# Attention beside an MLP on one core: w2's parts in fourteen tiles, the output weights split on GpSimd, other orders for attention

## The chip, the core and the metric

The kernel runs on one core of a Trainium2 chip. The core has five engines with a queue each: TensorE (PE; its weight loads are shown apart as PEld), VectorE (DVE), ScalarE (ACT), GpSimd (POOL) and SyncE (SP), which here issues nearly all DMAs. Each engine takes its instructions in order, and an instruction that has to wait holds up all behind it on that engine. Matmuls write to PSUM, which has eight banks of 128 partitions by 512 float32. The metric is the time of the kernel on the device in microseconds, less being better.

## The reference

Attention with 16 query heads that share one head of keys and values, and an MLP, both on the normalized input, are added to it. S = 2048 rows, D = 448, 16 heads of 28, F = 1792, all in float32:

```python
def _A_ref(x, wq, wk, wv, wo):
    q = (x @ wq).reshape(B, S, H, Dh).transpose(0, 2, 1, 3)
    k = x @ wk
    v = x @ wv
    scores = jnp.einsum("bhqd,bkd->bhqk", q, k) * (Dh ** -0.5)
    p = _softmax(scores, axis=-1)
    o = jnp.einsum("bhqk,bkd->bhqd", p, v)
    return o.transpose(0, 2, 1, 3).reshape(B, S, H * Dh) @ wo

def _B_ref(x, w1, b1, w2, b2):
    y = _layernorm(x, axis=-1)
    h = _gelu(jnp.einsum("bsd,df->bsf", y, w1) + b1)
    return jnp.einsum("bsf,fd->bsd", h, w2) + b2

xn = _layernorm(x, axis=-1)
return x + _A_ref(xn, A_wq, ...) + _B_ref(xn, B_w1, ...)
```

## The kernel before

The order of the work on every engine is the order in which the program writes it; nothing reorders it. Most products keep float32 accuracy by splitting both factors into a high part in a shorter format (fp32r) and the low rest: high x high, high x low and low x high are summed.

There are three stages. The first (to about 63 us) loads and normalizes the rows in four chunks of 512, splits the weights, and makes queries, keys and values; queries go to DRAM (`qd`) by DMA from tiles named `qe`.

**The MLP** (63 to 349 us) walks through 56 slots (loop at L635): four chunks of 512 rows by 14 tiles `ft` of the hidden width. In slot n, `mlp1` (L557) makes a hidden tile: eleven matmuls, then ScalarE, VectorE and GpSimd apply GELU and split the result into `hh` and `hl`. `mlp2` (L575) of two slots before multiplies `hh` and `hl` with w2: twelve matmuls. During the first chunk (c = 0), w2 is split too: `w2_split(s)` (L377) takes tiles 2s and 2s+1, 128 x 896 numbers. ScalarE writes the high part into `w2h`, VectorE the low part into `w2l`, and the load of part s+2 is issued (two buffers). It is called behind `mlp1` in slot 0 and in the odd slots 3, 5, ... 13 for s = 0 to 6, so that the parts s are first read by `mlp2` in slot 2s+2. `w2h` and `w2l` are one tile each of 14 x 448 columns; they lie in memory that the first stage's tiles held before.

**Attention** (from 349 us) has 16 units: four chunks of 512 queries by four groups of four heads. A unit walks through 16 key tiles of 128 keys. The steps of a unit are written out in a string of `ORDERS` (L34), where each word is a step:

- `s` with a number is `scores` (L612) of one key tile: three rounds of four matmuls (one for each head, on a quarter of the array's rows each) into four banks, then exponents on ScalarE (L625) into a tile `p`. The bits of the number say which neighbouring heads are joined in one instruction: bit 0 joins heads 0 and 1, bit 1 heads 1 and 2, bit 2 heads 2 and 3. So s6 makes one of 512 and one of 1536 columns, s5 two of 1024, s2 512, 1024, 512, s0 four of 512. Heads whose banks are not neighbours in number (7 and 0) aren't joined.
- `P` with a number is `weighted` (L791): the values are multiplied with the exponents of so many key tiles (`pv`, L735), summed in one bank, and VectorE adds the bank to `oc` (L733) or copies it for a unit's first (L731). A key tile is two rounds of four matmuls, on a quarter of the array's columns each.
- `m` searches the next unit's shift (`find_max`, L540: one matmul, L523, then four instructions on VectorE and a small DMA to the next unit's queries). `Q` is one output tile of the chunk before (`out_tile`, L703: twelve matmuls, L701). `T` and `E` are the same for the last chunk at the end of the kernel.

Banks are handed out in a ring of eight: four for a score step, one for each P, m, Q and T. A step waits for the bank that was handed out eight places before. Order 0 is for units 0 to 3, order 1 for units 4 to 14, order 2 for unit 15. Two score steps are made ahead of unit 0, so a unit's orders begin with the scores of its key tile 2 and end with the next unit's tile 1. A finished unit's normalization (`norm_jobs`, L711) is done by VectorE behind the first and third P of the next one, with one subtraction on GpSimd (`otl`, L723).

The output weights `wo` are loaded by four DMAs on SyncE's queue (L678) between the MLP and attention; the loads of unit 1's queries (`load_unit`, L533) stand behind them. `split_out` (L681) splits them on VectorE with a copy and a subtraction of 128 x 1792 numbers, behind the third step of unit 0. The parts are first read by Q in unit 4.

Of the kernel before, what the change touches and what calls it, by code (L numbers as in the profile page):

```python
# [11 lines left out]
F32R = mybir.dt.float32r  # L12
I32 = mybir.dt.int32
AF = mybir.ActivationFunctionType
ALU = mybir.AluOpType
# [3 lines left out]
P = 128  # L19
S, D, H, DH, F = 2048, 448, 16, 28, 1792  # L20
# [5 lines left out]
NF = F // P  # L26
# [4 lines left out]
MLP_ORDER = 1, 2, 3, 0  # L31
HD = D // 2
WEIGHTS = 7
ORDERS = ("s5 P1 s6 s6 P2 s6 s5 P2 s4 s1 m P2 s6 P1 s6 s5 P2 s6 s6 P2 s6 s5 P2 s6 s4 P2",  # L34
          "s5 P1 s6 s6 P2 s6 s5 P2 s6 s6 P2 s6 s5 P2 s2 s2 P2 s2 m Q s2 s6 P3 s6 s4 P2",
          "s5 P1 s6 s6 P2 s6 s5 P2 s6 s6 P2 s6 s5 P2 s2 s2 P2 s2 m Q s2 s6 P2 T T T E3")
FIRST_BANK = 0
LIMITS = 0.25, 2.0 ** 40

# [2 lines left out]
def block_kernel(ctx, tc, x, wq, wk, wv, wo, w1, b1, w2, b2, out):  # L42
    nc = tc.nc
    pe, act, dve, pool = nc.tensor, nc.scalar, nc.vector, nc.gpsimd
    ctx.enter_context(tc.manual_schedule())

    def f(t):
        return t.bitcast(F32)
# [60 lines left out]
    def bank(n, shape=(P, CW)):  # L109
        t = banks[0:shape[0], n, 0:shape[1] * (shape[2] if len(shape) > 2 else 1)]  # L110
        return t.rearrange("p (a b) -> p a b", b=shape[2]) if len(shape) > 2 else t
# [158 lines left out]
    def line(t):  # L270
        lines[t] = keep.tile([P, D], F32, name="a", bufs=4)
        nc.sync.dma_start(lines[t], xv[:, t, :])
# [99 lines left out]
    def w2_load(s):  # L372
        raw = rawtile([P, 2, D])
        nc.sync.dma_start(raw, w2[2 * s * P:(2 * s + 2) * P, :].rearrange("(b p) n -> p b n", p=P))
        wl_q.append(raw)

    def w2_split(s):  # L377
        raw = wl_q.pop(0)
        ab = slice(2 * s, 2 * s + 2)

        act.activation(w2h[:, ab, :], raw, AF.Copy, scale=0.5)
        dve.scalar_tensor_tensor(w2l[:, ab, :], raw, 0.5, f(w2h[:, ab, :]), op0=ALU.mult, op1=ALU.subtract)  # L382
        if s + 2 < NF // 2:
            w2_load(s + 2)

# [81 lines left out]
    for c in range(NCH):  # L467
        if c + 1 < NCH:
            center, turn = norm_parts(c + 1, False)
        for i in range(4):  # L470
# [4 lines left out]
            low = None  # L475
            if evac is not None:
                vt, low = evac()
# [3 lines left out]
            for part, k in (("", "c0 c1", "t0 c2 t1 c3", "t2 t3") if c == 0 else  # L481
                            ("c0 c1", "t0 c2 t1 c3", "t2 t3", "") if c + 1 < NCH else [""] * 4)[i].split():
                if part == "t" and low is not None:
                    low()
                    low = None
# [9 lines left out]
            if i in ((1, 3), (1, 2), (1, 3), (0, 2))[c]:  # L495
                n = 2 * c + (i - 1 if c == 1 else i // 2 if c == 3 else i // 3)
# [16 lines left out]
    def clear_q():  # L513
        both = xt_p.tile([P, 4, CW], F32R, name="xh")
        pool.memset(f(both), 0.0)
        qst.extend((both[:, 0:2, :], both[:, 2:4, :]))
# [16 lines left out]
    def load_unit(u):  # L533
        c, g = units[u]
        qs = qss[u] = qst[u % 2]
        for j in range(4):
            rs = slice(DH * (4 * g + j), DH * (4 * g + j + 1))
            nc.sync.dma_start(f(qs[32 * j:32 * j + DH, :, :]), qd[rs, :, c * CW:(c + 1) * CW])

    def find_max(u):  # L540
        mr = keep.tile([P, CW // 32], F32, name="mr", bufs=2)
        block_max(u, kd, mr)
        shift_rows(u, mr)
# [5 lines left out]

    ph1b = ExitStack()  # L550
    hp = ph1b.enter_context(tc.tile_pool(name="hp", bufs=3))
    w2h = hp.tile([P, NF, D], F32R, name="w2h", bufs=1)
    w2l = hp.tile([P, NF, D], F32R, name="w2l", bufs=1)

    hs, m2s = {}, {}

    def mlp1(c, ft):  # L557
        yh, yl = xts[MLP_ORDER[c], True]
        ph = spare()
        fs = slice(ft * P, (ft + 1) * P)  # L560
        proj(ph, lambda b: w1h[:, b, fs], lambda b: w1l[:, b, fs], yh, yl)
        hx = hrp.tile([P, CW], F32, name="hx", bufs=2)
        hz = hrp.tile([P, CW], F32, name="hz", bufs=2)
        act.activation(hx, ph, AF.Identity, bias=b1t[:, ft:ft + 1])  # L564
        act.activation(hz, ph, AF.Square, bias=b1s[:, ft:ft + 1], scale=GELU[0] ** 0.5)  # L565
        dve.scalar_tensor_tensor(hz, hz, 1.0, hx, op0=ALU.add, op1=ALU.mult)  # L566
        act.activation(hz, hz, AF.Tanh, scale=GELU[1])  # L567
        dve.scalar_tensor_tensor(hx, hz, 1.0, hx, op0=ALU.add, op1=ALU.mult)  # L568
        hh = hrp.tile([P, CW], F32R, name="hh")
        hl = hrp.tile([P, CW], F32R, name="hl")  # L570
        dve.tensor_copy(hh, hx)  # L571
        pool.tensor_sub(hl, hx, f(hh))  # L572
        hs[c, ft] = (hh, hl)

    def mlp2(c, ft, then=None):  # L575
        if ft == 0:
            m2s[c] = [bank(CT + k, (P, D)) for k in range(CT)]
        m2 = m2s[c]
        hh, hl = hs.pop((c, ft))
        terms = ((hh, w2h), (hh, w2l), (hl, w2h))  # L580
        parted = c == 0 and ft == 0
        if parted:
            for k in range(CT):
                for i, (h, w) in enumerate(terms[:2]):
                    pe.matmul(m2[k], h[:, k * P:(k + 1) * P], w[:, ft, :], start=(i == 0), stop=False)
        for k in range(CT):
            for i, (h, w) in enumerate(terms):
                if parted and i < 2:
                    continue
                pe.matmul(m2[k], h[:, k * P:(k + 1) * P], w[:, ft, :], start=(ft == 0 and i == 0),  # L590
                          stop=(ft == NF - 1 and i == 2))
            if ft == NF - 1:
                t = CT * MLP_ORDER[c] + k
                a = lines.pop(t)
                dve.tensor_add(a, a, m2[k])
                nc.sync.dma_start(ad[:, t, :], a)
            if then is not None:
                then(k)
# [13 lines left out]
    def scores(u, kt, joined):  # L612
        at = [bank_number() for j in range(4)]
        keys = slice(kt * P, (kt + 1) * P)
        for n, (i, h) in enumerate(((0, 0), (0, 1), (1, 0))):
            for j in range(4):
                rs = slice(32 * j, 32 * j + 32)
                pe.matmul(bank(at[j]), ks[rs, i, keys], qss[u][rs, h, :], start=(n == 0), stop=(n == 2))  # L618
        p = early.pop(0) if early else att.tile([P, 4, CW], F32, name=f"p{next(turn_p) % WEIGHTS}", bufs=1)
        j = 0  # L620
        while j < 4:
            n = 1
            while j + n < 4 and joined >> (j + n - 1) & 1 and at[j + n] == at[j] + n:
                n += 1
            act.activation(p[:, j:j + n, :], banks[:, at[j]:at[j] + n, :], AF.Exp, scale=SCALE)  # L625
            j += n
        ps[u, kt] = p
# [7 lines left out]
    for n in range(len(mslots) + 2):  # L635
        c, ft = mslots[n] if n < len(mslots) else (NCH, n - len(mslots))
        if 3 <= ft < 11 and ft % 2 and len(KEPT) <= c + 1 < NCH:
            line(CT * MLP_ORDER[c + 1] + (ft - 3) // 2)
        k = ft - (10 if c < NCH - 1 else 5)
        if c < NCH and 0 <= k < CT:  # L640
            line(CT * MLP_ORDER[c] + k)
        if c < NCH and 0 < k <= CT:
            a = lines[CT * MLP_ORDER[c] + k - 1]
            pool.tensor_add(a, a, b2b)
        if ft == 0 and 0 < c < NCH:
            a = lines[CT * MLP_ORDER[c - 1] + CT - 1]
            pool.tensor_add(a, a, b2b)
        if (c, ft) == (NCH - 1, 1):
            clear_q()
        if (c, ft) == (NCH - 1, 3):  # L650
            load_unit(0)
        if n < len(mslots):
            mlp1(c, ft)
        if c == 0 and (ft == 0 or ft % 2 and ft > 1):
            w2_split(ft // 2)
        if n in norms:
            norms[n]()
        if (c, ft) == (NCH - 1, 7):
            find_max(0)
        if n >= len(mslots):  # L660
            early.append(f(xl_p.tile([P, 4, CW], F32R, name="xl")))
            mlp2(*mslots[n - 2], then=lambda k: scores(*todo.pop(0), 5) if k == 0 else None)
        elif n >= 2:
            mlp2(*mslots[n - 2])
# [10 lines left out]
    wor = f(weights_tile())  # L675
# [3 lines left out]
    woh, wol = weights_tile(), weights_tile()  # L679

    def split_out():  # L681
        dve.tensor_copy(woh, wor)
        dve.tensor_sub(wol, wor, f(woh))


    sums = keep.tile([P, NU, CW // 32], F32, name="sums")
# [149 lines left out]
    for u in range(NU):  # L836
        if u + 1 < NU:
            load_unit(u + 1)
        if units[u][1] == 0 and u:
            load_rows_of(units[u][0] - 1)  # L840
        if u == NU - 2:
            load_rows_of(NCH - 1)
        for n, word in enumerate(ORDERS[(u >= NG) + (u == NU - 1)].split()):
            kind, times = word[0], int(word[1:] or 1)
            if kind == "s" and todo:
                scores(*todo.pop(0), times)
            elif kind == "P":
                weighted(times)
            elif kind == "E":
                last_burst(times, flag)  # L850
            else:
                token(kind, u)
            if (u, n) == (0, 2):
                split_out()
    outside = nc.values_load(count)
    with tc.If(outside > 0, preferred_fallthrough_block=True, label="outside"):
# [45 lines left out]
```

## Time and profile before

| | us |
|---|---|
| median of 3 runs | 894.08 (893.58 to 894.96) |
| the profiled execution's own time | 893.52 |
| its span, first to last instruction | 891.7 |
| TensorE busy | 875.2 |
| ScalarE busy | 650.1 |
| VectorE busy | 360.7 |
| GpSimd busy | 155.3 |
| scores' matmuls (L618), busy | 256.1 |
| P's matmuls (L739), busy | 243.4 |
| exponents (L625), busy | 484.8 |

In the views of the profile, a row of a timeline begins with its start and its length in microseconds, then engine, line, operation, and what it writes and reads; xN are N merged instructions, and square brackets hold the engine's idle time just before and what ended it. The chain of waits follows the work that ended last backwards; its pieces begin with start and length too. A row of the waits names who waited and for whom, then microseconds in total, times, and the longest. In rows of groups stand busy time and mean nanoseconds of one, then idle time before. "issue" is time in which an engine waited for nothing that the profile shows. TensorE's granted clock was 0.997 of full speed on the mean.

### The profile page before, as it was taken

The page shows a single profiled execution, that of the slowest core. Times are in us where ns is not written, and L with a number is a line of the kernel's source. Part 1 is how long each engine was busy: PE and PEld are TensorE (multiplying, and loading weights), DVE is VectorE, ACT ScalarE, POOL GpSimd, SP SyncE. Part 2 cuts the span into 40 slices and gives each one's busy share as a digit, 9 for nine tenths or more (in the row PEclk, how much of TensorE's full clock was granted, in tenths as well). Part 3 has the DMA queues.
Part 4 walks back from the last instruction along what each step waited for, and adds up shares of the span by engine and source line. Part 5 has one row for each costly group of instructions (what it writes and reads, how often), then busy time and mean ns, then how long its engine had stood idle before and what let it go on. Part 6 is the DMA issues. An engine that isn't in the chain of part 4 may idle for free.

```text
span 891.7 us, 16976 instructions
## 1 busy us (share of the span) xinstructions
PE 875.2 (98%) x6997; PEld 529.5 (59%) x6997; DVE 360.7 (40%) x654; ACT 650.1 (73%) x890; POOL 155.3 (17%) x149
## 2 busy tenths in 40 slices
PE   9999999999999999899999999999999999999997
PEld 8877888888888886333434444444444444444444
DVE  7865454335345353342343234233233233333323
ACT  5765443333443436799999898898898899899891
POOL 7443243242234332000000000000000000000000
PEclk9999999999999999999999999999999999999999
DMA  9792112002001103000002101102101102102001
GB/s 301 215 288 81 42 63 83 1 1 83 21 21 51 44 11 91 9 22 22 9 16 64 33 1 33 33 2 74 32 1 33 33 1 74 33 1 73 12 1 54
DMA packets 28957, 46.02 MB, mean 52 GB/s; under 512 B 4542, under 2 KB 20492, under 8 KB 28876
## 3 DMA queue, kind: packets, MB, share of 16 engines
q1 hardware_dynamic: 27468, 44.32, 16.1%
q8 instruction: 56, 0.92, 0.4%
q10 hardware_dynamic: 1408, 0.57, 0.2%
q14 instruction: 25, 0.20, 0.1%
HBM read 28.22 MB, written 14.68 MB: 48 GB/s over the span
## 4 chain that ended last, share of the span: by engine, by line
PE 87%; ACT 7%; issue 2%; DVE 2%; DMA 1%; SPq 0%; DVEq 0%; ACTq 0%
PE banks L618 24%; PE banks L739 23%; PE banks L180 15%; PE banks L590 15%; ACT p L625 5%; PE banks L701 4%; PE banks L185 2%; PE banks L183 2%; PE banks L304 1%; PE banks L523 1%; DMA xl<-in_A_wo_dram 1%; DMA qd<-qe 0%; DVE w2l L382 0%; PE banks L776 0%; DMA rows<-in_A_x_dram 0%
## 5 line engine op out<-in xcount | busy, mean ns | idle before, releaser
L625 ACT ACTIVATE p<-banks 128x1024 f32<-128x1024 f32 (+2 forms) x623 | 484.8, 879 | 39.5 <-PE banks L618 36.4
L618 PE MATMUL banks<-xh,ks 32*128 32x512 f32 x3072 | 256.1, 424 | 6.4 <-DVE oc L733 4.3
L618 PEld LDWEIGHTS banks<-xh,ks 32*128 32x128 f32 x3072 | 145.0, 183 | 168.0 <-ACT p L625 142.7
L739 PE MATMUL banks<-p,vs 128*32 128x512 f32 x2008 | 243.4, 601 | 0.0
L733 DVE TENSOR_TENSOR oc<-oc,banks 128x512 f32<-128x512 f32 x115 | 78.9, 686 | 304.0 <-PE banks L739 245.9
L739 PEld LDWEIGHTS banks<-p,vs 128*32 128x32 f32 x2008 | 52.2, 109 | 120.9 <-issue 80.4
L564 ACT ACTIVATE hx<-banks,b1t 128x512 f32<-128x512 f32 x56 | 38.5, 688 | 110.7 <-PE banks L185 103.7
L572 POOL TENSOR_TENSOR hl<-hx,hh 128x512 fp32r<-128x512 f32 x56 | 76.8, 1371 | 182.3 <-DVE hh L571 176.9
L723 POOL TENSOR_TENSOR otl<-oc,oth 128x512 fp32r<-128x512 f32 x15 | 19.2, 1280 | 487.7 <-DVE oth L722 487.7
L566 DVE SCALAR_TENSOR_TENSOR hz<-hz,hx 128x512 f32<-128x512 f32 x56 | 44.3, 792 | 101.6 <-ACT hz L565 101.3
L590 PE MATMUL banks<-w2l,hh 128*128 128x448 f32 x220 | 81.0, 368 | 0.8 <-DVE w2l L382 0.7
L590 PE MATMUL banks<-w2h,hl 128*128 128x448 f32 x224 | 81.4, 366 | 0.0
L590 PE MATMUL banks<-w2h,hh 128*128 128x448 f32 x220 | 81.0, 368 | 0.1
L567 ACT ACTIVATE hz<-hz 128x512 f32<-128x512 f32 x56 | 35.4, 632 | 48.5 <-DVE hz L566 48.5
L180 PE MATMUL banks<-xl,w1h 128*128 128x512 f32 x168 | 65.7, 391 | 0.0
L180 PE MATMUL banks<-xh,w1l 128*128 128x512 f32 x168 | 65.6, 391 | 0.0
L180 PE MATMUL banks<-xh,w1h 128*128 128x512 f32 x168 | 65.5, 390 | 0.0
L568 DVE SCALAR_TENSOR_TENSOR hx<-hz,hx 128x512 f32<-128x512 f32 x56 | 39.1, 698 | 42.9 <-ACT hz L567 42.9
L590 PEld LDWEIGHTS banks<-w2l,hh 128*128 128x128 f32 x220 | 41.3, 188 | 7.1 <-DVE w2l L382 3.2
L590 PEld LDWEIGHTS banks<-w2h,hh 128*128 128x128 f32 x220 | 41.3, 188 | 6.0 <-issue 0.7
L590 PEld LDWEIGHTS banks<-w2h,hl 128*128 128x128 f32 x224 | 42.1, 188 | 3.3
L565 ACT ACTIVATE hz<-banks,b1s 128x512 f32<-128x512 f32 x56 | 38.2, 682 | 0.0
(156 smaller groups left out, 765.3 us busy)
## 6 DMA issues: line engine op xcount, KB each, us to landing
xh<-qd SPq DMA_DIRECT2D x64, 112.0 KB
qd<-qe SPq DMA_DIRECT2D x12, 512.0 KB
a<-in_A_x_dram SPq DMA_DIRECT2D x24, 224.0 KB
ad<-a SPq DMA_DIRECT2D x16, 224.0 KB
row<-ad SPq DMA_DIRECT2D x16, 224.0 KB
raw<-in_B_w_dram SPq DMA_DIRECT2D x7, 448.0 KB
out_dram<-row SPq DMA_DIRECT2D x14, 224.0 KB
ks<-qe SPq DMA_DIRECT2D x16, 112.0 KB
```

What stands on the lines that cost most here:

```text
L180: pe.matmul(ps, w, v, start=(n == 0), stop=False)
L564: act.activation(hx, ph, AF.Identity, bias=b1t[:, ft:ft + 1])
L565: act.activation(hz, ph, AF.Square, bias=b1s[:, ft:ft + 1], scale=GELU[0] ** 0.5)
L566: dve.scalar_tensor_tensor(hz, hz, 1.0, hx, op0=ALU.add, op1=ALU.mult)
L568: dve.scalar_tensor_tensor(hx, hz, 1.0, hx, op0=ALU.add, op1=ALU.mult)
L572: pool.tensor_sub(hl, hx, f(hh))
L590: pe.matmul(m2[k], h[:, k * P:(k + 1) * P], w[:, ft, :], start=(ft == 0 and i == 0), stop=(ft == NF - 1 and i == 2))
L618: pe.matmul(bank(at[j]), ks[rs, i, keys], qss[u][rs, h, :], start=(n == 0), stop=(n == 2))
L625: act.activation(p[:, j:j + n, :], banks[:, at[j]:at[j] + n, :], AF.Exp, scale=SCALE)
L701: pe.matmul(po, ots[c, g][o][:, ts], w[:, g, :], start=(n == 1), stop=(stop and n == 3 * len(gs)))
L733: dve.tensor_add(pos[u], pos[u], po)
L739: pe.matmul(po[32 * j:32 * j + 32, :], vs[:, k, :], ps[u, k][:, j, :], start=(k == kt), stop=(k == kt + n - 1))
```

## The change

It has three parts. w2's high and low parts lie in seven pairs of tiles of two hidden tiles each, and are split in the even slots 0, 2, ... 12 of the first chunk. `split_out` runs on GpSimd (a multiplication by one in place of the copy, then the subtraction) and is issued behind the third step of unit 2. The three orders are other ones: order 0 has sixteen times one score step and a P1; order 1 begins with eight such steps, keeps P2 and P3 around Q, and ends with one more; order 2 begins as order 1.

```diff
-ORDERS = ("s5 P1 s6 s6 P2 s6 s5 P2 s4 s1 m P2 s6 P1 s6 s5 P2 s6 s6 P2 s6 s5 P2 s6 s4 P2",
-          "s5 P1 s6 s6 P2 s6 s5 P2 s6 s6 P2 s6 s5 P2 s2 s2 P2 s2 m Q s2 s6 P3 s6 s4 P2",
-          "s5 P1 s6 s6 P2 s6 s5 P2 s6 s6 P2 s6 s5 P2 s2 s2 P2 s2 m Q s2 s6 P2 T T T E3")
+ORDERS = ("s2 P1 s4 P1 s2 P1 s2 P1 s1 P1 m s2 P1 s4 P1 s2 P1 s2 P1 s2 P1 s4 P1 s4 P1 s4 P1 s2 P1 s2 P1 s2 P1",
+          "s2 P1 s2 P1 s2 P1 s2 P1 s2 P1 s4 P1 s4 P1 s0 P1 s6 P2 s4 s4 m Q s0 s1 P3 s6 s4 P2 s2 P1",
+          "s2 P1 s2 P1 s2 P1 s2 P1 s2 P1 s4 P1 s4 P1 s0 P1 s6 P2 s4 s4 m Q s0 s1 P3 s6 T T T E3")
...
     def w2_split(s):
         raw = wl_q.pop(0)
-        ab = slice(2 * s, 2 * s + 2)
-
-        act.activation(w2h[:, ab, :], raw, AF.Copy, scale=0.5)
-        dve.scalar_tensor_tensor(w2l[:, ab, :], raw, 0.5, f(w2h[:, ab, :]), op0=ALU.mult, op1=ALU.subtract)
+        high, low = w2s[s]
+        act.activation(high, raw, AF.Copy, scale=0.5)
+        dve.scalar_tensor_tensor(low, raw, 0.5, f(high), op0=ALU.mult, op1=ALU.subtract)
         if s + 2 < NF // 2:
             w2_load(s + 2)
...
-    w2h = hp.tile([P, NF, D], F32R, name="w2h", bufs=1)
-    w2l = hp.tile([P, NF, D], F32R, name="w2l", bufs=1)
+    w2s = [[hp.tile([P, 2, D], F32R, name=f"w2{n}{s}", bufs=1) for n in "hl"] for s in range(NF // 2)]
...
-        terms = ((hh, w2h), (hh, w2l), (hl, w2h))
+        high, low = (w[:, ft % 2, :] for w in w2s[ft // 2])
+        terms = ((hh, high), (hh, low), (hl, high))
...
-        if c == 0 and (ft == 0 or ft % 2 and ft > 1):
+        if c == 0 and ft % 2 == 0:
             w2_split(ft // 2)
...
     def split_out():
-        dve.tensor_copy(woh, wor)
-        dve.tensor_sub(wol, wor, f(woh))
+        pool.tensor_scalar(woh, wor, 1.0, 0.0, op0=ALU.mult, op1=ALU.add)
+        pool.tensor_sub(wol, wor, f(woh))
...
-            if (u, n) == (0, 2):
+            if (u, n) == (2, 2):
                 split_out()
```

More of the change, by code (lines that the diff above doesn't have):

```diff
@@ L584, in mlp2 @@
                 for i, (h, w) in enumerate(terms[:2]):
-                    pe.matmul(m2[k], h[:, k * P:(k + 1) * P], w[:, ft, :], start=(i == 0), stop=False)
+                    pe.matmul(m2[k], h[:, k * P:(k + 1) * P], w, start=(i == 0), stop=False)
         for k in range(CT):
@@ L589, in mlp2 @@
                     continue
-                pe.matmul(m2[k], h[:, k * P:(k + 1) * P], w[:, ft, :], start=(ft == 0 and i == 0),
+                pe.matmul(m2[k], h[:, k * P:(k + 1) * P], w, start=(ft == 0 and i == 0),
                           stop=(ft == NF - 1 and i == 2))
```

## The prediction, made before the change was run

> **What bounds the kernel now.** First the page: its span, the busy time of the engines, and the chain that ended last.
>
> ```profile
> span 891.7 us, 16976 instructions
> PE 875.2 (98%) x6997; PEld 529.5 (59%) x6997; DVE 360.7 (40%) x654; ACT 650.1 (73%) x890; POOL 155.3 (17%) x149
> PE 87%; ACT 7%; issue 2%; DVE 2%; DMA 1%; SPq 0%; DVEq 0%; ACTq 0%
> ```
>
> TensorE is busy nearly throughout and has the chain, but ends of matmuls are modelled, so this is not 98% of its peak. ScalarE has 7% of the chain, so places exist where exponents set the pace. I look for them stage by stage: MLP, start of attention, attention's rhythm.
>
> The chain in order of time, in the MLP (one nine-matmul group starts each slot):
>
> ```profile
> 74.80 2.04 PE banks L180 x9
> ...
> 92.45 2.69 PE banks L590 x12
> ...
> 97.64 2.43 PE banks L590 x12
> ...
> 136.57 2.09 PE banks L180 x9
> 141.55 2.05 PE banks L180 x9
> ...
> 200.81 2.05 PE banks L180 x9
> ```
>
> Once w2 is split, twelve slots take 200.81 - 141.55 = 59.26 us. While it is being split, twelve take 136.57 - 74.80 = 61.77, and every other second matmul takes 2.69 instead of 2.43. So 2.5 us are lost there. The waits name who is late, and the timeline shows the first case:
>
> ```profile
> PEld banks L590 <- DVE w2l L382: 3.2, 6, 1.1
> 69.82 0.95 ACT L381 ACTIVATE w2h<-raw 128x896 fp32r<-128x896 f32 x1 [1.15 <-DMA qd<-qe]
> ...
> 72.31 0.47 PE L585 MATMUL banks<-w2l,hh 128*128 128x448 f32 x1 [1.01 <-DVE w2l L382]
> ```
>
> Six times TensorE waits for w2's low part, because a pair of tiles split in an odd slot is used in the next slot. The first split waits 1.15 us for a DMA out of the memory that w2h takes over, and TensorE then waits 1.01 us.
>
> At the start of attention, the timelines of VectorE and TensorE:
>
> ```profile
> 356.64 1.09 DVE L682 CAST xl<-xl 128x1792 fp32r<-128x1792 f32 x1 [4.94 <-DMA xl<-in_A_wo_dram]
> ...
> 359.81 0.68 DVE L733 TENSOR_TENSOR oc<-oc,banks 128x512 f32<-128x512 f32 x1
> 354.74 1.49 PE L618 MATMUL banks<-xh,ks 32*128 32x512 f32 x15
> 360.54 1.48 PE L618 MATMUL banks<-xh,ks 32*128 32x512 f32 x9 [4.31 <-DVE oc L733]
> ...
> 364.88 1.91 PE L618 MATMUL banks<-xh,ks 32*128 32x512 f32 x24
> ```
>
> VectorE stands in front of the output weights' DMA, the sum (L733) queued behind the split holds a PSUM bank until 360.49, and TensorE, which stopped for 4.31 us, goes on 0.05 later.
>
> Then the rhythm, from TensorE's timeline: the first step of order 0, two later steps, and unit 4.
>
> ```profile
> 348.91 0.97 PE L618 MATMUL banks<-xh,ks 32*128 32x512 f32 x12
> 349.80 1.07 PE L739 MATMUL banks<-xl,vs 128*32 128x512 f32 x8
> 350.80 2.16 PE L618 MATMUL banks<-xh,ks 32*128 32x512 f32 x24
> ...
> 481.49 2.14 PE L618 MATMUL banks<-xh,ks 32*128 32x512 f32 x24
> ...
> 500.76 0.96 PE L618 MATMUL banks<-xh,ks 32*128 32x512 f32 x12
> ...
> 504.51 1.74 PE L618 MATMUL banks<-xh,ks 32*128 32x512 f32 x24
> 506.22 2.78 PE L739 MATMUL banks<-p,vs 128*32 128x512 f32 x24
> 508.93 1.92 PE L618 MATMUL banks<-xh,ks 32*128 32x512 f32 x24
> 510.78 1.92 PE L739 MATMUL banks<-p,vs 128*32 128x512 f32 x16
> 512.64 0.97 PE L618 MATMUL banks<-xh,ks 32*128 32x512 f32 x12
> ```
>
> A score step reaches its P after 0.90 us (348.91 to 349.80). From P to the next score it is 1.00 for P1, 1.86 for P2, 2.71 for P3. So "s P1" costs 1.895 us of TensorE. Two scores reach their P after 1.71 (504.51 to 506.22), so the second adds 0.80, and a pair with its P2 needs 1.71 + 1.86 = 3.57, or 1.78 per key tile. But from 481.49 to 500.76 five such pairs took 19.27: 1.93 per key tile. TensorE's bare work is smaller in pairs, yet pairs wait. For what? ScalarE's timeline:
>
> ```profile
> 609.65 1.45 ACT L625 ACTIVATE p<-banks 128x1536 f32<-128x1536 f32 x1
> 610.99 0.60 ACT L625 ACTIVATE p<-banks 128x512 f32<-128x512 f32 x1
> ...
> 611.94 1.06 ACT L625 ACTIVATE p<-banks 128x1024 f32<-128x1024 f32 x1
> 571.61 0.60 ACT L625 ACTIVATE p<-banks 128x512 f32<-128x512 f32 x1 [1.69 <-PE banks L618]
> 570.55 1.75 PE L618 MATMUL banks<-xh,ks 32*128 32x512 f32 x24
> ```
>
> The next start comes 1.34 us after one with 1536 columns, and 0.475 after one with 512 (two of them lie between 610.99 and 611.94): 0.43 per 512 columns and about 0.05 per instruction. The last two rows give 1.06 us from a score's start to its first exponent.
>
> **The change part by part.** All against the profiled execution's own 893.52 us (span 891.7 and 1.8 around it).
>
> *w2's splits, one slot earlier (2s instead of 2s+1, used from slot 2s+2).* The same seven instructions per engine; ScalarE has to spare in a slot. The low part is ready about a slot (4.94 us) early against a lateness of at most 1.1. All 2.5 us go: **-2.5**. Each next load is issued a slot earlier and lands four slots before its use. What would be late next is hl from GpSimd, in time in the twelve steady slots.
>
> *Fourteen tiles instead of two.* Pair 0's split no longer waits for the DMA unless its own 7 KB lie on that DMA's source. If it goes, w2h starts 1.15 earlier, w2l at 69.87 after hh, and the 1.01 of TensorE goes. Ends: 0 and -1.3; I take **-1.0**, since a tile a seventh as large probably misses it.
>
> *Output weights out of unit 0.* From 354.74 to 364.88 the pair took 10.14 instead of 3.85: **-6.3**. GpSimd's price, from the nearest rows:
>
> ```profile
> L723 POOL TENSOR_TENSOR otl<-oc,oth 128x512 fp32r<-128x512 f32 x15 | 19.2, 1280 | 487.7 <-DVE oth L722 487.7
> ```
>
> At 1.28 us per 512 columns, 1792 take 4.5, two of them at most 9. GpSimd idled 487.7 us before this line, the next in its queue is such an otl, first read in unit 4, 31 us or more later: 0. What if the cover were gone: at most 9 us once.
>
> *What is late next in unit 0.* The search for unit 1's maximum moves from the eighth score to the fifth. It comes at 348.91 + 4 x 1.895 + 1.9 = 358.4, and stands in TensorE's queue. It needs unit 1's queries, which SyncE issues behind the four wo DMAs. DMA traffic of 349 to 360 in 40 slices:
>
> ```profile
> GB/s 182 378 326 398 339 378 391 176 72 241 280 300 202 189 176 163 189 228 189 176 176 191 184 182 179 238 179 186 238 209 142 37 15 7 7 7 0 0 0 0
> ```
>
> Data flow until slice 36, 358.9, and the last arrival still has to be signalled: a new wait of 0.5 to, as an estimate, 1.2, of which I take the long end: **+1.1**. In later units the load is issued before the unit begins.
>
> *Orders.* Order 0 becomes sixteen "s P1". TensorE needs 1.895 each. ScalarE, in three instructions (512, 1024, 512), needs 4 x 0.43 + 3 x 0.05 = 1.87, in four 1.92. Does the ring of eight banks let TensorE run free? A step takes five banks, so the last head of score n+1 goes where score n's first head was: free at 1.06 + 0.60 + 0.05 = 1.71 after score n began, needed at 1.895. P of n takes the bank of score n-1's second head: free 2.65 after that began (1.06 + 0.48 + 1.06 + 0.05), needed at 1.895 + 0.90 = 2.80. P's sum (0.68 on VectorE) ends about 1 us before its bank is needed. So the least slack is 0.15 us, and TensorE sets the pace. The maximum adds, with the next two rows:
>
> ```profile
> 366.72 0.51 PE L523 MATMUL banks<-xh,kd 128*128 128x512 f32 x1
> 367.16 1.92 PE L739 MATMUL banks<-p,vs 128*32 128x512 f32 x16
> 397.83 0.49 PE L523 MATMUL banks<-xh,kd 128*128 128x512 f32 x1
> ...
> 460.08 0.49 PE L523 MATMUL banks<-xh,kd 128*128 128x512 f32 x1
> ```
>
> 0.44. Unit: 16 x 1.895 + 0.44 = 30.76; now (460.08 - 397.83)/2 = 31.12. Four units: **-1.45**.
>
> Order 1 begins with eight "s P1", 15.16 us. From there, counting from score 9: P2 at 0.90; score 10 at 2.75 and 11 at 3.55, whose last head waits 0.12 for P2's sum; the maximum at 4.5; Q at 5.0, 0.15 late behind an exponent; score 12 at 7.51, 13 at 8.31; P3 at 9.23; score 14 at 11.94, 15 at 12.74 (0.15 late); P2 at 13.67; score 16 at 15.52, P1 at 16.42, the next unit at 17.42. Sum 32.58. ScalarE idles 0.9, 1.0 and 0.6 us in it, between P2 and score 10, in Q, and in P3; more would be hidden there. The units of now, by the Q's on the chain:
>
> ```profile
> 502.15 2.43 PE banks L701 x12
> ...
> 832.85 2.43 PE banks L701 x12
> ```
>
> 330.70 over ten units: 33.07. Eleven units gain 0.49 each: **-5.4**. The last unit has the same steps up to its last score, which I count like another: **-0.5**; the tail behind is unchanged.
>
> Sum: -2.5 - 1.0 - 6.3 + 1.1 - 1.45 - 5.4 - 0.5 = -16.05, so 877.5 on the profiled execution. The median of the runs shown is 894.08, 0.56 above it: **878.0**.
>
> The rule that speaks against this change: the Trainium skill, ScalarE: Activation LUTs, section What ACT_TABLE_LOAD costs, says that an ACTIVATE with immediate operands takes 186 ns plus 0.833 ns per column and that neighbours overlap by 93 ns. By it each chained instruction costs 0.093 us beside its columns, not 0.05, a step of three 1.985 us, and the sum would be 892, as in the first rival. The trace agrees with it for one exponent of 512 columns (0.60 us, the rule 0.61), not for the distance of two (0.475, the rule 0.52).
>
> **The rivals.** *ScalarE sets the pace.* The new orders, laid on the ring of banks, make 796 exponents of the 623 now, since a joined group that wraps round the ring is cut. One of 512 columns takes 0.60, 0.17 beside its 0.43 of columns; chained, 0.05 of that stays. If in the new mix half of the 0.17 stayed, 0.09, a step would take 1.99, 0.09 above TensorE's, and 64 + 88 + 8 = 160 such steps would give back 14.4 us: 892, just below before. For: ScalarE is at 1.87 of 1.895. Against: 0.05 is read between chained exponents. 7%. The figure of the Trainium skill quoted above would do this.
>
> *The ring closes (slower).* If the first exponent begins or frees its bank over 0.15 us later than I add up, the last head waits in each "s P1", and the lateness comes back in every step: 160 x 0.05 is 8 us for each 0.05. From 0.10 beyond the slack the whole gain is gone; at 0.2 it is 910. For: pairs wait in just this way now, and TensorE has four more changes between scores and P per unit (1.00 against 0.85 for a key tile within a P). Against: 0.15 is three times the 0.05 of a semaphore. Slower 9%; a part of it, 881 to 891, 14%.
>
> *The parts do nothing.* w2's wait stays where it is or the stall merely moves to the maximum: 2.5 + 1.0 + 1.2 given back, 882. 8%.
>
> **How the numbers follow.** Forecast as summed, 874 to 882: 62%. Its terms' ends (first split 0 to -1.3, the new wait 0.5 to 1.2, a tenth of a microsecond per unit either way) make about 4. The range takes in the rival of unmoved waits and most of the partly closed ring: 873 to 889. Differences within 0.2%, 1.8 us, cannot be told from none. Same: a third of the ScalarE rival and the edge of the ring, 5%. Slower 9%. Faster the rest, 86%.
>
> **What would show it.** In the MLP even slots of 4.94 and no L590 waiting for w2l; in unit 0 no stop at 356 but one of about 1 us before the first L523; between L523 of units 1 to 3 30.8 us; Q's 32.6 apart; scores in "s P1" 1.895 apart with no wait on ACT ahead of them. Steps of 2.0 with ScalarE without gaps would be the first rival; steps above that with gaps on both engines the second. Wrong altogether: if a P1 behind a P1's score cost more than the 1.895 of the single steps from which I took it, since none follows another now.

## The result, and the profile after

The changed kernel takes 885.68 us (median of four runs, 884.61 to 886.08) against 894.10 for the kernel before (four runs, 893.58 to 894.96): a ratio of 0.9901, with a 95% interval from 0.9886 to 0.9915. The forecast was 878.0 with a range from 873 to 889. So the sign and the range hold, but the gain is 8.4 us where the sum gave 16.

The profiled execution took 885.42 us. The page of the changed kernel, its span, the engines' busy time and the chain that ended last by engine:

```profile
span 883.6 us, 17299 instructions
...
PE 869.4 (98%) x6997; PEld 513.5 (58%) x6997; DVE 412.4 (47%) x727; ACT 654.0 (74%) x1063; POOL 161.4 (18%) x151
...
PE 93%; DVE 2%; DMA 1%; ACT 1%; issue 1%; SPq 1%; ACTq 0%; DVEq 0%
```

ScalarE's share of the chain fell from 7% to 1%, though it now has 173 instructions more. The span fell by 8.1 us. Cut at the scores that open each unit (the first of its order), the two traces divide it like this, lengths in us:

| stretch | before | after | difference | forecast |
|---|---|---|---|---|
| up to the MLP's first slot | 63.33 | 63.70 | +0.4 | none |
| slot 2, w2's first use | 6.33 | 6.39 | +0.1 | -1.0 |
| slots 4, 6, ... 14 in all | 32.11 | 29.64 | -2.5 | -2.5 |
| unit 0 | 37.33 | 31.81 | -5.5 | -5.6 |
| unit 1 | 31.04 | 34.23 | **+3.2** | -0.4 |
| units 2 and 3 | 62.31 | 61.54 | -0.8 | -0.7 |
| units 4 to 14 | 363.74 | 361.59 | **-2.2** | -5.4 |
| unit 15 and the end | 48.39 | 47.62 | -0.8 | -0.5 |

(The forecast for unit 0 is the stall's -6.3, the new wait's +1.1 and order 0's -0.36.) Three rows carry nearly the whole error: slot 2, unit 1, and units 4 to 14.

**The MLP.** The chain of the changed kernel, one nine-matmul group per slot (line numbers are one or two lower than before):

```profile
75.24 2.05 PE banks L180 x9
80.18 2.06 PE banks L180 x9
85.12 2.06 PE banks L180 x9
...
134.52 2.06 PE banks L180 x9
```

Each slot takes 4.94, from the second used pair on, and no wait of L589 for w2's low part is left among the waits. The first pair is another matter. Slot 2 in the timeline:

```profile
70.59 0.95 ACT L380 ACTIVATE w2h<-raw 128x896 fp32r<-128x896 f32 x1 [1.55 <-DMA qd<-qe]
...
72.73 0.48 PE L584 MATMUL banks<-w2l,hh 128*128 128x448 f32 x1 [0.66 <-DVE w2l L381]
```

The split still waits for the DMA out of `qe`, and TensorE behind it for both parts.

**Unit 0.** TensorE's timeline, from the first step to behind the search for the maximum:

```profile
346.84 0.97 PE L617 MATMUL banks<-xh,ks 32*128 32x512 f32 x12
347.74 1.06 PE L738 MATMUL banks<-xl,vs 128*32 128x512 f32 x8
348.73 0.97 PE L617 MATMUL banks<-xh,ks 32*128 32x512 f32 x12
...
355.31 1.07 PE L738 MATMUL banks<-p,vs 128*32 128x512 f32 x8
357.43 0.47 PE L522 MATMUL banks<-xh,kd 128*128 128x512 f32 x1 [1.06 <-DMA xh<-qd]
```

A step is 1.89 us (346.84 to 348.73) with no idle time. The stall of the output weights is gone, and the one that was forecast in its place, in front of the maximum, is there with 1.06 us.

**Unit 1.** VectorE, GpSimd, TensorE and ScalarE in the timeline; a bracket holds the idle time before the row:

```profile
388.65 1.70 POOL L681 TENSOR_SCALAR xl<-xl 128x1792 fp32r<-128x1792 f32 x1
...
389.04 0.71 DVE L523 STREAM_TRANSPOSE tm<-banks 128x512 f32<-128x512 f32 x1
389.78 0.69 DVE L524 TENSOR_REDUCE mr<-tm 128x16 f32<-128x512 f32 x1
390.43 4.00 POOL L682 TENSOR_TENSOR xl<-xl 128x1792 fp32r<-128x1792 f32 x1
390.50 3.96 DVE L528 TENSOR_SCALAR mn<-mr 128x16 fp32r<-128x16 f32 x1
394.50 0.71 DVE L529 STREAM_TRANSPOSE tm<-mn 128x512 f32<-128x512 f32 x1
395.14 1.47 DVE L732 TENSOR_TENSOR oc<-oc,banks 128x512 f32<-128x512 f32 x2
395.84 0.96 PE L617 MATMUL banks<-xh,ks 32*128 32x512 f32 x10 [2.90 <-DVE oc L732]
396.68 5.51 ACT L624 ACTIVATE p<-banks 128x512 f32<-128x512 f32 x8 [3.06 <-PE banks L617]
```

GpSimd's queue was empty, so it did the split, which stands in the program behind the third step of unit 2, in unit 1 already. While its subtraction ran (390.43 to 394.43), an instruction of VectorE with 16 columns, a step of the maximum, took 3.96 us and ended 0.03 behind it. A transpose and two sums stood behind it in VectorE's queue, the banks that the sums read came free late, TensorE stopped for 2.90 us and ScalarE for 3.06. The same instruction takes 0.17 or 0.18 us in the fifteen other searches of this trace.

**Later.** Between the searches of units 2 and 3, in TensorE's timeline:

```profile
422.34 0.50 PE L522 MATMUL banks<-xh,kd 128*128 128x512 f32 x1
...
453.13 0.49 PE L522 MATMUL banks<-xh,kd 128*128 128x512 f32 x1
```

30.79 apart: order 0 keeps the counted 30.76. In order 1, the Q's on the chain:

```profile
527.44 2.61 PE banks L700 x12
...
855.80 2.63 PE banks L700 x12
```

(855.80 - 527.44) / 10 = 32.84, not 32.6. TensorE's timeline of unit 5 from its ninth score on shows where:

```profile
522.38 0.97 PE L617 MATMUL banks<-xh,ks 32*128 32x512 f32 x12
523.27 1.92 PE L738 MATMUL banks<-p,vs 128*32 128x512 f32 x16
525.13 1.89 PE L617 MATMUL banks<-xh,ks 32*128 32x512 f32 x24
...
529.98 1.80 PE L617 MATMUL banks<-xh,ks 32*128 32x512 f32 x24
531.71 2.78 PE L738 MATMUL banks<-p,vs 128*32 128x512 f32 x24
534.42 1.91 PE L617 MATMUL banks<-xh,ks 32*128 32x512 f32 x24
536.25 1.92 PE L738 MATMUL banks<-p,vs 128*32 128x512 f32 x16
...
540.00 0.97 PE L617 MATMUL banks<-xh,ks 32*128 32x512 f32 x12
```

Counted from 522.38, score 10 comes at 2.75 (counted 2.75), score 12 at 7.60 (7.51), P3 at 9.33 (9.23), P2 at 13.87 (13.67), the next unit at 17.62 (17.42). A tenth is lost around Q and a tenth in the last pair.

### The profile page after: what moved, and what is told of

It reads as the page before. It is cut to its first block, busy times and chain, and to the rows that moved or that the text cites. A ratio compares the mean times of both kernels' runs of the same rounds, so it can differ in the third digit from the quotient of the medians.

```text
span 883.6 us, 17299 instructions
## 1 busy us (share of the span) xinstructions
PE 869.4 (98%) x6997; PEld 513.5 (58%) x6997; DVE 412.4 (47%) x727; ACT 654.0 (74%) x1063; POOL 161.4 (18%) x151
## 4 chain that ended last, share of the span: by engine, by line
PE 93%; DVE 2%; DMA 1%; ACT 1%; issue 1%; SPq 1%; ACTq 0%; DVEq 0%
PE banks L738 27%; PE banks L617 25%; PE banks L180 16%; PE banks L589 15%; PE banks L700 4%; PE banks L185 2%; PE banks L183 2%; PE banks L304 1%; PE banks L522 1%; DMA xh<-qd 1%; DMA qd<-qe 0%; DVE mn L528 0%; ACT p L624 0%; PE banks L775 0%; DMA kvraw<-in_A_wv_dram 0%
## 5 line engine op out<-in xcount | busy, mean ns | idle before, releaser
L624 ACT ACTIVATE p<-banks 128x512 f32<-128x512 f32 (+2 forms) x796 | 488.8, 780 | 30.3 <-PE banks L617 30.0
L738 PE MATMUL banks<-p,vs 128*32 128x512 f32 x2008 | 257.7, 602 | 0.0
L617 PE MATMUL banks<-xh,ks 32*128 32x512 f32 x3072 | 246.6, 421 | 3.0 <-DVE oc L732 2.9
L617 PEld LDWEIGHTS banks<-xh,ks 32*128 32x128 f32 x3072 | 135.7, 183 | 193.0 <-issue 93.6
L732 DVE TENSOR_TENSOR oc<-oc,banks 128x512 f32<-128x512 f32 x190 | 130.4, 686 | 243.1 <-PE banks L738 228.9
L738 PEld LDWEIGHTS banks<-p,vs 128*32 128x32 f32 x2008 | 44.9, 108 | 101.9 <-ACT p L624 54.2
L589 PE MATMUL banks<-w2h,hl 128*128 128x448 f32 x224 | 81.5, 366 | 0.0
L589 PE MATMUL banks<-w2h,hh 128*128 128x448 f32 x220 | 81.1, 369 | 0.1
L589 PE MATMUL banks<-w2l,hh 128*128 128x448 f32 x220 | 80.5, 366 | 0.0
L589 PEld LDWEIGHTS banks<-w2h,hh 128*128 128x128 f32 x220 | 41.4, 188 | 5.9 <-issue 0.7
L589 PEld LDWEIGHTS banks<-w2h,hl 128*128 128x128 f32 x224 | 42.1, 188 | 3.3
L589 PEld LDWEIGHTS banks<-w2l,hh 128*128 128x128 f32 x220 | 41.4, 188 | 4.1
```

The costliest lines, as they stand in the source:

```text
L589: pe.matmul(m2[k], h[:, k * P:(k + 1) * P], w, start=(ft == 0 and i == 0), stop=(ft == NF - 1 and i == 2))
L732: dve.tensor_add(pos[u], pos[u], po)
L738: pe.matmul(po[32 * j:32 * j + 32, :], vs[:, k, :], ps[u, k][:, j, :], start=(k == kt), stop=(k == kt + n - 1))
```

## The experiments

The first theory on unit 1 is that VectorE's small instruction cannot run while GpSimd's subtraction does. The rival is that the split, wherever it stands, delays something else (traffic, a queue, the readers of the weights). The other experiments take up the two further misses, and the steps that came out right for perhaps the wrong reason. Most of these kernels were run once, beside the kernel before at 894.7 to 895.0; two were run four and five times. Single totals are rough (four runs of the first experiment's kernel lie between 880.80 and 884.25), so the argument goes by the lengths of units and slots in the traces. All but the split on VectorE and the split in pieces also have the first experiment's edit, and are compared with its 881.38.

**The split in unit 4**, where order 1 has its maximum far from it:

```diff
-            if (u, n) == (2, 2):
+            if (u, n) == (4, 5):
                 split_out()
```

> The output weights' split stays on GpSimd as it is, but is issued in unit 4 behind its third P (behind otl of unit 3) instead of in unit 2. Theory 1 (an exclusive hold: the maximum's small VectorE instruction mn, L528, waits until GpSimd's 4.0 us subtraction ends): in unit 4 no such instruction runs beside the subtraction, so unit 1's 34.2 us become 30.75 and unit 4 stays at 32.8; the whole is 3.4 us faster than the changed kernel, about 882. Theory 2 (any 5.7 us of GpSimd work on 128x1792 slows the attention loop, wherever it lies): the 3.4 us move to unit 4, which then takes about 36, and the whole stays at 885.5.

One run: 881.38 us. Unit 1 takes 30.84 instead of 34.23, and unit 4 takes 32.83, as in the changed kernel (32.81). Its timeline:

```profile
390.02 0.17 DVE L528 TENSOR_SCALAR mn<-mr 128x16 fp32r<-128x16 f32 x1
...
480.38 1.69 POOL L681 TENSOR_SCALAR xl<-xl 128x1792 fp32r<-128x1792 f32 x1
482.16 4.04 POOL L682 TENSOR_TENSOR xl<-xl 128x1792 fp32r<-128x1792 f32 x1
```

The same two instructions of GpSimd, no shorter, now cost nothing, and VectorE's takes 0.17. Beside the subtraction VectorE's sums (L732, which read a bank) ran in their usual 0.69 us, so the loss needs those two instructions beside each other, the subtraction and the one of 16 columns. The same kernel once more:

> The kernel of e1 once more, timed in rounds. Expected: 881.4 within 0.7, and below the changed kernel's 884.6 to 886.1 by the 3.4 us of unit 1.

It takes 882.03 us (median of four runs, 880.80 to 884.25) against 894.66 before, ratio 0.9855 (0.984 to 0.9871). The median is where it was expected, the spread is wider. The profiled run is the longest of the four, and its ScalarE shows where that one lost its time:

```profile
71.04 0.95 ACT L380 ACTIVATE w2h<-raw 128x896 fp32r<-128x896 f32 x1 [2.37 <-DMA qd<-qe]
```

The first split of w2 waited 2.37 us instead of the 1.15 in the run of 881.38, TensorE's granted clock then was 0.59 and 0.56 in the stretches from 74 to 76 and 76 to 78 us (1.00 in the other run), and slots 2 and 3 took 13.76 us instead of 11.26: 2.5 of the 2.9 us between the two runs.

**The split in unit 2 on VectorE again:**

```diff
-        pool.tensor_scalar(woh, wor, 1.0, 0.0, op0=ALU.mult, op1=ALU.add)
-        pool.tensor_sub(wol, wor, f(woh))
+        dve.tensor_copy(woh, wor)
+        dve.tensor_sub(wol, wor, f(woh))
```

> The split in unit 2 as in the changed kernel, but on VectorE again (copy 1.1 and subtraction 2.0 us). Theory 1 says nothing is held then: mn in unit 1 takes 0.17 us and unit 1 30.75, but the sum of unit 2's second P stands behind 3.1 us of split and 1.1 us of normalization, about 2 us past the moment when its bank is needed, so unit 2 takes about 32.7 instead of 30.75: 1.4 us faster than the changed kernel, about 884. Theory 2 has no say on VectorE's own queue, but would also expect 30.75 in unit 1.

One run: 883.57 us; unit 1 takes 30.84, unit 2 32.50 instead of 30.72. TensorE's timeline there:

```profile
416.88 0.96 PE L617 MATMUL banks<-xh,ks 32*128 32x512 f32 x10 [1.30 <-DVE oc L732]
```

VectorE's own copy and subtraction ahead of the sums stop TensorE too, for 1.30 us, and cost 1.8 us. At this place in the program VectorE was the cheaper engine (GpSimd's price was 3.4).

**GpSimd's two instructions in four pieces each**, at the place of the change:

```diff
-        pool.tensor_scalar(woh, wor, 1.0, 0.0, op0=ALU.mult, op1=ALU.add)
-        pool.tensor_sub(wol, wor, f(woh))
+        for g in range(NG):
+            pool.tensor_scalar(woh[:, g], wor[:, g], 1.0, 0.0, op0=ALU.mult, op1=ALU.add)
+        for g in range(NG):
+            pool.tensor_sub(wol[:, g], wor[:, g], f(woh[:, g]))
```

> The split on GpSimd in the changed kernel's place, but each of its two instructions cut into four of 448 columns (about 0.5 and 1.1 us each). Theory 1 with the hold given up after each instruction: mn waits at most 1.1 us, which the slack of the next sums nearly covers, so unit 1 takes 30.8 to 31.3, 883. If the hold is kept across neighbouring GpSimd instructions, or if it is the amount of GpSimd work that counts (theory 2): unit 1 stays at 34 or gets longer.

One run: 882.50 us, unit 1 30.85. The timeline of GpSimd and VectorE:

```profile
388.89 2.16 POOL L682 TENSOR_SCALAR xl<-xl 128x448 fp32r<-128x448 f32 x4
...
390.75 0.33 DVE L528 TENSOR_SCALAR mn<-mr 128x16 fp32r<-128x16 f32 x1
391.01 4.47 POOL L684 TENSOR_TENSOR xl<-xl 128x448 fp32r<-128x448 f32 x4
```

GpSimd works 6.6 us instead of 5.7, in the same place, and VectorE's instruction takes 0.33. It began while the last piece of the first instruction ran (to 391.05) and ended 0.03 behind it, where the whole subtraction held it for 3.96 us. So it is not a busy GpSimd that holds this instruction of VectorE, but the one instruction that GpSimd is in when it starts, until that one's end. How long a piece of the subtraction (about 1.1 us) would hold it no run shows; here none met it. (Unit 0 took 32.32, with a wait of 1.53 us for the queries in front of the maximum; this lies ahead of the split.)

**Wide exponents in order 0.** The ring arithmetic gave 0.15 us of slack to the joins that the change has. With s6 in every step ScalarE has less to do, but the heads of its 1536 columns free their banks together and late:

```diff
-ORDERS = ("s2 P1 s4 P1 s2 P1 s2 P1 s1 P1 m s2 P1 s4 P1 s2 P1 s2 P1 s2 P1 s4 P1 s4 P1 s4 P1 s2 P1 s2 P1 s2 P1",
+ORDERS = ("s6 P1 s6 P1 s6 P1 s6 P1 s6 P1 m s6 P1 s6 P1 s6 P1 s6 P1 s6 P1 s6 P1 s6 P1 s6 P1 s6 P1 s6 P1 s6 P1",
```

> The kernel of e1 with every score step of order 0 as s6 (exponents of 512 and 1536 columns, cut where the group wraps round the ring) in units 0 to 3. ScalarE then has 0.05 us less work per step. If the ring's arithmetic of the prediction holds, P of step n waits for the 1536-column exponent of step n-1: free 3.05 us after that score began, so the step becomes (3.05 + 1.0)/2 = 2.02 us in the six of eight ring positions where it isn't cut, and units 2 and 3 take about 32.3 instead of 30.75. If ScalarE's amount of work set the pace, they would take 30.75 or less.

One run: 887.78 us. Units 0 to 3 take 32.84, 32.57, 32.30 and 32.75, where the change's joins gave 31.71, 30.84, 30.72 and 30.82. TensorE's timeline:

```profile
428.31 0.97 PE L617 MATMUL banks<-xh,ks 32*128 32x512 f32 x12
429.21 1.07 PE L738 MATMUL banks<-p,vs 128*32 128x512 f32 x8
430.21 0.97 PE L617 MATMUL banks<-xh,ks 32*128 32x512 f32 x12
431.37 1.06 PE L738 MATMUL banks<-p,vs 128*32 128x512 f32 x8 [0.19 <-ACT p L624]
432.37 0.96 PE L617 MATMUL banks<-xh,ks 32*128 32x512 f32 x12
```

Steps of 1.90 and of 2.16 follow each other, the longer ones with a wait for exponents. The P at 431.37 goes on 0.05 us behind the 1536-column exponent of the score that began at 428.31. It doesn't multiply these exponents (its own are of a score before that, since two are made ahead); it takes a bank that this exponent read. It is the ring that closes here and not ScalarE's amount of work, which is smaller (1008 instructions on the page, against 1063). The rival that the prediction called "the ring closes" is real, and begins where the joins are wider.

**Narrow exponents in order 0**, every head its own instruction (s0 in all sixteen steps), which measures ScalarE's fixed cost:

```diff
-ORDERS = ("s2 P1 s4 P1 s2 P1 ...
+ORDERS = ("s0 P1 s0 P1 s0 P1 s0 P1 s0 P1 m s0 P1 s0 P1 s0 P1 s0 P1 s0 P1 s0 P1 s0 P1 s0 P1 s0 P1 s0 P1 s0 P1",
```

> The kernel of e1 with every score step of order 0 as s0, four exponents of 512 columns, in units 0 to 3. With 0.05 us per chained instruction beside the columns a step is 4 x 0.478 = 1.91 plus 0.02 for the wait at its start, so ScalarE is just behind TensorE's 1.895 and units 2 and 3 take about 31.2 instead of 30.75. With 0.093 per instruction (the figure of the Trainium skill) a step would be 2.08 and the units 33.3 to 33.6.

One run: 885.17 us; units 1 to 3 take 31.51 each, a little above the 31.2 that was expected. ScalarE's timeline, then TensorE's:

```profile
410.39 8.28 ACT L624 ACTIVATE p<-banks 128x512 f32<-128x512 f32 x16
```

```profile
410.81 1.03 PE L617 MATMUL banks<-xh,ks 32*128 32x512 f32 x12
...
412.77 1.03 PE L617 MATMUL banks<-xh,ks 32*128 32x512 f32 x12
```

ScalarE has no gap, and a step is 1.96 us. Four exponents make 0.49 each: 0.43 for the columns and 0.06 fixed, against 0.05 in the prediction. (The row's 8.28 us end with the whole of the last exponent, which has 0.94 here because it begins before the one ahead of it has ended; the sixteen starts lie 7.35 / 15 = 0.49 apart.) The Trainium skill's rule that the prediction weighed (ScalarE: Activation LUTs, section What ACT_TABLE_LOAD costs) would give 0.52 each and a step of 2.08; the measurement decides for the row.

**The old orders**, with the rest of the change:

```diff
-ORDERS = ("s2 P1 s4 P1 s2 P1 ...
+ORDERS = ("s5 P1 s6 s6 P2 s6 ...
```

> The kernel of e1 with the three orders of the kernel before. This prices the new orders alone. From the two profiles: units 1 to 3 at 31.1 instead of 30.8, units 4 to 14 at 33.07 instead of 32.87, unit 15 with the tail 0.8 longer, unit 0 at 31.0 since the maximum comes late enough for its load: 0.9 + 2.2 + 0.8 - 0.7 = 3.2 us slower than e1, about 884.6. By the prediction's own hand count it would be 1.1 + 5.4 + 0.5 - 0.7 = 6.3 slower, about 887.7.

One run: 884.48 us, 3.1 above the first experiment's 881.38. Of this, units 4 to 14 make 2.1 (363.59 against 361.45), the end 0.7, and units 0 to 3 only 0.4, as the new order has the wait for the queries and the old one has not. Forecast for the orders were 1.45 + 5.4 + 0.5 less the wait of 1.1, so 6.25.

**w2's first pair in a tile of its own pool.** Was the miss in slot 2 a matter of size, as the prediction put it? The built program's memory map puts the first pair where the first rows lay, and on no `qe` tile; it waits all the same. So perhaps the wait belongs to the pool (the stretch of memory out of which a stage's tiles are handed out, opened and closed as a whole): its first tile waits for the last use of the pool whose memory it takes over. Here the pair is taken out of that pool and put into the first rows' own tile:

```diff
+    front = ph1.enter_context(tc.tile_pool(name="front", bufs=1))
...
-        first_raw = wqp.tile([P, CT, D], F32, name="rows", bufs=2)
+        first_raw = (wqp if c else front).tile([P, CT, D], F32, name="rows", bufs=1)
...
-    w2s = [[hp.tile([P, 2, D], F32R, name=f"w2{n}{s}", bufs=1) for n in "hl"] for s in range(NF // 2)]
+    pair0 = front.tile([P, CT, D], F32R, name="rows", bufs=1)
+    w2s = [[pair0[:, 0:2, :], pair0[:, 2:4, :]]]
+    w2s += [[hp.tile([P, 2, D], F32R, name=f"w2{n}{s}", bufs=1) for n in "hl"] for s in range(1, NF // 2)]
```

> The kernel of e1, with pair 0 of w2 in a pool of its own that was opened before the first stage's pool and takes the place of the first chunk's rows there (same bytes, other pool; the rest of the fourteen tiles as before). Theory 1 (the first split waits because the MLP's pool as a whole follows the first stage's pool, whichever bytes a tile has): pair 0 waits no more for the last DMA from qe, w2h is written right behind the first tanh (1.5 us earlier), slot 2 takes 5.0 to 5.2 instead of 6.33, and the whole is 1.2 us faster than e1, about 880.2. Theory 2 (the wait is for its own data or for a counter that is shared with that DMA): slot 2 stays at 6.33 and the whole at 881.4.

One run: 880.74 us. Slot 2 takes 4.94 instead of 6.33, slot 3 5.20. The timeline:

```profile
68.68 0.94 ACT L381 ACTIVATE rows<-raw 128x896 fp32r<-128x896 f32 x1
...
70.10 2.01 POOL L573 TENSOR_TENSOR hl<-hx,hh 128x512 fp32r<-128x512 f32 x1 [4.24 <-DVE hh L572]
...
70.88 1.78 DVE L567 SCALAR_TENSOR_TENSOR hz<-hz,hx 128x512 f32<-128x512 f32 x1
```

The split has no wait left, with bytes of the same former owner: the wait went with the pool and not with the bytes. Attention begins 1.0 us earlier (345.48 against 346.46); 0.6 of that is left in the total of one run, beside single units that differ by 0.1 to 0.3 either way.

**Fourteen tiles or two.** The first experiment with w2's parts in two tiles as before, but split in the even slots:

```diff
-    w2s = [[hp.tile([P, 2, D], F32R, name=f"w2{n}{s}", bufs=1) for n in "hl"] for s in range(NF // 2)]
+    w2h = hp.tile([P, NF, D], F32R, name="w2h", bufs=1)
+    w2l = hp.tile([P, NF, D], F32R, name="w2l", bufs=1)
+    w2s = [[w[:, 2 * s:2 * s + 2, :] for w in (w2h, w2l)] for s in range(NF // 2)]
```

> The kernel of e1 with w2's parts in two tiles again, as before, but split in the even slots. Theory 1 (only the earlier slot counts, since readers wait for the slices that they read and not for whole tiles): slots 4 to 14 take 4.94 as with fourteen tiles, and the whole 881.4. Theory 2 (a reader of one pair waits for the write of the next pair into the same tile): even slots get longer again by 0.3 to 1.1 us, 883.5 to 885.

One run: 882.42 us, within the four runs of the first experiment's kernel. Slots 4 to 14 take 4.94 each, slot 2 6.53. So the number of tiles did nothing that shows; the earlier slot did all of the 2.5 us.

**The output weights' loads behind unit 1's queries:**

```diff
-    for j in range(4):
-        nc.sync.dma_start(wor[32 * j + 1:32 * j + 1 + DH, :, :], wo.rearrange(...)[j])
...
             load_unit(u + 1)
+        for j in range(4 if u == 0 else 0):
+            nc.sync.dma_start(wor[32 * j + 1:32 * j + 1 + DH, :, :], wo.rearrange(...)[j])
```

> The kernel of e1, with the four DMAs of the output weights issued behind the load of unit 1's queries instead of ahead of it. If unit 0's new wait ahead of the maximum (unit 0 takes 31.7, units 2 and 3 30.75) comes from that load standing behind wo, unit 0 takes 30.8 and the whole is 0.9 us faster than e1, 880.5. If it comes from something else at the start of attention (the sums of the MLP, the first exponents), unit 0 stays at 31.7.

One run: 880.74 us; unit 0 takes 30.75 instead of 31.71. TensorE's timeline, where the maximum now follows without idle time:

```profile
355.01 1.06 PE L736 MATMUL banks<-p,vs 128*32 128x512 f32 x8
356.01 0.50 PE L522 MATMUL banks<-xh,kd 128*128 128x512 f32 x1
```

The new wait was the place of the queries in SyncE's queue, and it was worth 1.0 us in unit 0 (0.6 in the total of one run).

**The three together** (split in unit 4, first pair apart, weights' loads behind):

> The changed kernel with e1, e5 and e6 together: the split in unit 4, pair 0 in a pool of its own, wo's DMAs behind unit 1's queries. They touch slot 2 and 3, unit 0 and units 1 and 4, so their gains should add: 3.4 + 1.0 + 0.9 off 885.7, 880.4, or 0.985 of the kernel before. If unit 0's maximum waits for another thing once wo is out of its way, unit 0 stays above 30.9 and the whole at 881.

It takes 879.64 us (five runs, 879.20 to 879.84) against 894.66 before (nine runs): ratio 0.9834 (0.9821 to 0.9848). It beats both kernels, and the 880.4 that was expected. In its profile unit 0 takes 30.72, unit 1 30.72 and slot 2 4.94. Its runs lie within 0.64 us of each other, where those of the first experiment's kernel spread over 3.45; that the missing waits for DMAs make them steadier is likely, but nine runs don't show it.

## Why the prediction was half right

**w2's splits, one slot earlier: right.** -2.5 was forecast, -2.5 measured, all from the slot.

**"A tile a seventh as large probably misses it": wrong.** The forecast of -1.0 took the wait for one of overlapping bytes. The tile does miss the DMA's source and waits nevertheless, since its pool takes over the memory of another one. It was the same in the kernel before: by that program's memory map, `w2h`, whose write waited, lies on no `qe` tile (only `w2l` does), so smaller tiles could not help. With another pool the term is 1.0 to 1.4 us (attention begins 1.0 earlier, slot 2 is 1.4 shorter); in the change it was 0.

**Output weights out of unit 0: right**, with the wait that takes its place: unit 0 fell by 5.5 where -6.3, +1.1 and -0.36 were forecast, and with the weights' loads behind the queries just that wait goes.

**GpSimd's price of "0": the step that failed most.** The prediction named its cover: "GpSimd idled 487.7 us before this line" and the next reader is far away. GpSimd's time is indeed free. But the question was what else runs beside it, and one instruction of VectorE could not. The cost is 34.23 - 30.84 = 3.4 us, below the "at most 9 us once" that stood there for lost cover, but that price was in neither the sum nor the range. The prediction also reckoned from the place in the program, unit 2; an idle engine ran ahead to unit 1, to the middle of the search for the maximum. The Trainium skill has the rule that was overlooked. SBUF — State Buffer, section Who interferes with whom, says that VectorE and GpSimd share a pair of ports which one of them holds for a whole instruction, that a `tensor_scalar` on VectorE can be in a mode that needs it, and that a `tensor_reduce` never contends. The trace agrees: 3.96 us beside a subtraction of 4.00, 0.33 beside pieces, 0.17 alone, and the reduction at 389.78 ran its 0.69 us beside GpSimd's first instruction. In which mode VectorE's instruction ran, no run here shows.

**Order 0: right.** 30.76 was counted, 30.72 and 30.82 measured in units 2 and 3; "s P1" has its 1.895, and the wide exponents bear out the arithmetic of the ring behind its slack: it gave 32.3 for units 2 and 3, and 32.30 and 32.75 were measured.

**Order 1: right in its mechanism, mis-sized.** 0.49 a unit was the difference of two numbers near 33. The old one, read from the chain, was right (33.07). The new one, added up by hand from single rows, was 0.19 too small (32.77 in unit 5 against 32.58), and this is over a third of the gain, eleven times: 2.1 us. Which of the single rows were too short stays open beyond the two places named above. About 1.1 more comes from units that took up to 0.44 longer than unit 5 (361.59 - 11 x 32.77), 0.8 of it from units 8 and 12. There one step is 0.3 to 0.4 longer than in its neighbours. In unit 8 VectorE's sum behind P3 starts 0.40 us after the wait for it is over, at 633.44, for nothing that the profile shows. With the split on VectorE, unit 8 has no such gap and takes 32.83, so it is no part of order 1. What it is was not tried, and stays open.

**The rivals.** "ScalarE sets the pace" falls: the fixed cost is 0.05 to 0.06 between chained exponents, and even four instructions a step cost 1.96, not 1.99 with three. "The ring closes" did not happen, but would have with other joins. "The parts do nothing" holds for one of its parts, the first split. The total lay in the range because the range reached to partly lost gains; none of the cases named there was the one that came. That is luck: three misses, of 1.1, 3.6 and 3.2 us, happened to stay within what had been allowed for other cases.

## What to carry to other kernels

An engine that idles is not free to use: before work goes to GpSimd, look at which VectorE instructions will run beside it at the time at which it will really run (as soon as its queue is empty and its operands are there), and keep long GpSimd instructions away from short VectorE ones that others wait for, or cut them in pieces. Held here was a `tensor_scalar` between two SBUF tiles; a transpose, a reduction and sums out of PSUM were not. A gain that is the difference of two nearly equal counts, many times over, deserves its error worked out per unit. And where a wait names a DMA on memory that is taken over, ask whether it hangs on the tile or on the pool.

## What was not expected of the hardware

A VectorE instruction on 128x16 numbers took 3.96 us instead of 0.17 while GpSimd subtracted, while the transpose out of PSUM and the reduction that ran beside GpSimd's first instruction took 0.71 and 0.69, as they do elsewhere. The same kind of hold is likely in slot 2 of the kernel with w2's first pair apart, where `hz` (two operands in SBUF) took 1.78 us, against 0.69 for the same line one hidden tile earlier; GpSimd's `hl` ran from 70.10 to 72.11, and `hz` from 70.88 to 72.66. That this is the same hold was not tested by itself.
